# Top-32 attention and two MLPs on one core: the attention output moves from the score banks into the h banks of PSUM

## The chip, the cores and the metric

One core of one Trainium2 chip runs the whole kernel. The metric is the device time of one execution in microseconds (us); lower is better. The core's engines are named as in the profile: PE (matrix multiply; PEld is its weight load), DVE, ACT, POOL and SP, which here only issues DMAs. PSUM, the memory that PE writes, has eight banks of 512 fp32 columns on 128 partitions; SBUF is the working memory.

## The reference

For 4 batches of 8 heads, 576 tokens and head size 64:

```python
scores = (1 / sqrt(64)) * q @ k.T
kth    = the 32nd largest score of each row
scores = where(scores >= kth, scores, -1e9)
attn   = exp(scores - rowmax);  attn = attn / (attn.sum(-1) + 1e-9)
x      = attn @ v                                   # (2304 tokens, 512)
h      = x @ w_in;  g = maximum(0.01 * h, h);  y = g @ w_out
z      = maximum(maximum(y @ w1, y @ w2), y @ w3);  out = z @ w2_out
```

The first MLP is 512 to 2048 to 512, the second 512 to 768 (three times) to 512. Everything is fp32 in the reference.

## The kernel before

**Numbers.** PE works in fp16: each fp32 operand is scaled, split into a high and a low fp16 half, and each product is three matmuls (high by high, high by low, low by high). In `three` these are lines 876 to 878, in the attention output lines 833 to 835.

**Attention.** The tokens of a batch are cut into four blocks of 128 and one of 64. A step of `attention(i)` takes one block and two heads (the block of 64: four heads, laid on the two halves of the partitions), 72 steps in all. In a step:

- In two rounds, j = 0 and 1, PE writes the scores of 128 rows (one head, or two heads of the block of 64) into the tile `s` (line 718), and ACT copies them to `S` in SBUF (line 723). There is one `s` tile, so the scores of j = 1 wait for the copy of j = 0.
- DVE finds the 32nd largest score of each row: four MAX8 and three MATCH_REPLACE8 per j (lines 738, 740).
- ACT takes the exponential (788), DVE and POOL mask it (793, 797, 800), ACT and POOL split it (802, 804) into `phl`, and a DMA transposes it into `pt` (807).
- PE multiplies `pt` by `vt` (833 to 835): 30 matmuls a head pair. `vt` has a 65th column of ones, so each head gives 64 outputs and the row's sum in column 64.
- DVE adds 1e-9 to the sums, read from PSUM (line 840), and takes the reciprocal (842). ACT reads each head's 64 columns from PSUM, scales them by the reciprocal and writes them to `xs` (844). ACT and POOL split `xs` into `xhl` (850, 852).

After the last head of a block a DMA transposes `xhl` into `xu`, the input of the MLPs.

**The MLPs.** `ffn(u)` takes ten units of up to 256 tokens: an H phase (w_in, one `h` tile per 128 outputs, evacuated by ACT, line 924), accumulation with w_out in `acc`, an M phase (w1, w2, w3: three `h` tiles per 128 outputs, evacuated by ACT, line 1017, and DVE, line 1021), and accumulation with w2_out in `acc` again. The weights are unpacked and split by DVE, ACT and POOL in the first part of the kernel, beside the first attention steps.

**PSUM before.** Two banks form one tile, `sav`: the scores take columns 0 to 287 of each bank, the attention output (`av`) columns 288 to 417. Two banks are `acc`, four are `h`, which serves the H and M phases, the weight preparation and small sums (`total`, line 315).

**Order of the work.** Nothing is ordered by hand. `Plan` collects every operation with an engine, a cost, a priority and what it reads and writes, simulates the five engines and writes the instructions in the order of its start times. What the plan keeps apart are its own buffers: `s` and `av` are two buffers to it, although they lie in one tile. The semaphore waits are set afterwards, by the tile framework, from the tiles that instructions touch. The table `NB` says how many buffers a tag has; `hH`, `hM` and `hW` limit how many of the four `h` banks one phase may hold (`fbuf`). `RLAG` is a time by which the plan holds back line 840 after its input is ready.

Of the kernel before, what the change touches and what calls it, by code (L numbers as in the profile page):

```python
# [9 lines left out]
F32 = mybir.dt.float32  # L10
# [4 lines left out]
AF = mybir.ActivationFunctionType  # L15
ALU = mybir.AluOpType
# [11 lines left out]
PS = 2048.0  # L28
LNPS = float(np.log(PS))
P = 128  # L30
# [11 lines left out]
PE, ACT, DVE, POOL, SP = "PE", "ACT", "DVE", "POOL", "SP"  # L42
# [29 lines left out]
class Plan:  # L72
# [13 lines left out]
    def op(self, eng, dur, fn, r=(), w=(), pr=0.0, dma=0.0, lag=0.0):  # L86
        n = Node()
        n.eng, n.dur, n.fn, n.pr, n.dma, n.lag = eng, dur, fn, pr, dma, lag
        n.succ, n.ready, n.idx, n.eps = [], 0.0, len(self.nodes), self.eps
        deps, n.bufs = set(), []  # L90
        for k in r:
            if k in self.lastw:
                deps.add(self.lastw[k])
            self.readers.setdefault(k, []).append(n.idx)
        for k in w:
            deps.update(self.readers.get(k, ()))
            if k in self.lastw:
                deps.add(self.lastw[k])
        for k in w:
            self.lastw[k] = n.idx  # L100
            self.readers[k] = []
        deps.discard(n.idx)
        for k in list(r) + list(w):
            k = k[0] if isinstance(k, tuple) else k
            for b in (k, *k.also) if isinstance(k, Buf) else ():
                if b not in n.bufs:
                    n.bufs.append(b)
                    b.left += 1
                    b.emit += 1
        n.nd = len(deps)  # L110
        self.nodes.append(n)
        for d in deps:
            self.nodes[d].succ.append(n)
        return n
# [88 lines left out]
def act(n, psum=False, aps=0):  # L203
    return (n * 0.833 + (70 if psum else 120) + 105 * aps) / 1000
# [15 lines left out]
def attention_moe_kernel(ctx, tc, qk, v, w_in, w_out, w123, w2o, outT):  # L220
    nc = tc.nc
    V, G, A, T, Y = nc.vector, nc.gpsimd, nc.scalar, nc.tensor, nc.sync
# [3 lines left out]
    ps = ctx.enter_context(tc.tile_pool(name="ps", bufs=1, space=bass.MemoryType.PSUM))  # L226
# [2 lines left out]

    NB = {"xu": 2, "raw": 2, "hl": 1, "k2": 7, "kt": 4, "qt": 2, "vt": 4, "S": 3, "w": 1, "m": 2, "nb": 2, "pp": 1,  # L230
          "phl": 1, "pt": 1, "r": 2, "xs": 1, "xhl": 1, "f16t": 4, "yj": 1,
          "s": 1, "av": 1, "acc": 2, "h": 4, "junk": 1, "xcap": 2, "pr": 8, "ph": 4, "ra": 3, "fi": 6, "ft": 9, "rw": 3, "fz": 3, "rc": 2, "hH": 2, "hM": 3, "hW": 1, "kH": 2, "kM": 5, "fH": 2, "fM": 2}
    PSUM_TAGS = ("s", "av", "acc", "h")
    plan = Plan(NB, {"raw", "av", "junk", "hl", "k2", "h", "f16t", "rc"})
    op = plan.op
    cnt = [0]

    def buf(tag, shape, dt=F32):
        pl = ps if tag in PSUM_TAGS else sb

        def make():
            cnt[0] += 1
            if tag in ZONE:
                return ZONE[tag].pop(0)
            return pl.tile(shape, dt, tag=tag, bufs=NB[tag], name=f"{tag}_{cnt[0]}")

        b = plan.buf(tag, make)
        if tag in ZONE:
            b.done = lambda: ZONE[tag].append(b.ap)
        return b  # L250

    def fbuf(tag, ph, shape, dt=F32):
        b = buf(tag, shape, dt)
        b.also = (plan.buf({"h": "h", "k2": "k", "f16t": "f"}[tag] + ph, lambda: 1),)
        return b
# [20 lines left out]
            "ph": [wof[:, 11264 + 1152 * i:12416 + 1152 * i].rearrange("p (a s) -> p a s", a=2) for i in range(4)],  # L276
            "fz": [w2f[:, 1536 * e:1536 * e + 1536].bitcast(I32) for e in range(1, 4)]}
    NCOL = 318
    sav = ps.tile([P, 2, 512], F32, name="sav")
    ZONE["s"] = [sav[:, :, :288]]  # L280
    ZONE["av"] = [sav[:, :, 288:418]]
    colt = cp.tile([P, NCOL], F32, name="colt")
    cpos = [0]

# [392 lines left out]
        return TE + TS * i if i < NE else TA0 + TA * i  # L677

    EXPP = 4
    RLAG = 3.0  # L680
    COLD = 1.7
    NCOLD = 8
    FM = 1
# [12 lines left out]
    def attention(i):  # L696
        s = steps[i]
        b, t0, n, hps = s["b"], s["t0"], s["n"], s["hps"]
        full = n == P
        pr = TP(i)  # L700
# [42 lines left out]
        else:  # L743
# [6 lines left out]
            for x, g in [(0, 0), (0, 1), (1, 0), (0, 2), (1, 1), (0, 3), (1, 2), (0, 4), (0, 5), (0, 6)]:  # L750
# [13 lines left out]
               pr=pd)  # L764
# [46 lines left out]
        if blk not in XHL:  # L811
            XHL[blk] = buf("xhl", [P, 2, HP, P], F16)
        xhl = XHL[blk]
        xs = buf("xs", [P, 4, 64])
        avb = buf("av", [P, 512])
        av = lambda: avb().rearrange("p x (h e) -> p x h e", e=65)
        avh = lambda a: av()[:, a // 2, a % 2] if not full else av()[:, 0, a]
        for j in range(2):
            vt = VT[b, hps[j]]

            def avm(j=j, vt=vt):
                hs = [(j, slice(0, P), j)] if full else [(hh, slice(64 * hh, 64 * hh + 64), 2 * j + hh)
                                                        for hh in range(2)]
                for hh, qs, a in hs:
                    o = avh(a)[:qs.stop - qs.start, :]
                    for c in range(5):
                        if c < 4:
                            ch, k = c + 5 * j, 2 * c + hh
                        else:
# [7 lines left out]
            op(PE, 15 * mm(64) * (1 if full else 2) * (COLD if i < NCOLD else 1), avm, r=[pt] + [(vt, x) for x in range(3)], w=[avb, (xs, "a"), (xhl, "a", i)], pr=pa)  # L837
        nh = 2 if full else 4
        r = buf("r", [P, 8])
        op(DVE, 0.07, lambda: V.tensor_scalar(r()[:n, 0:nh].rearrange("p (x h) -> p x h", h=2),  # L840
                                             av()[:n, 0:nh // 2, :, 64], 1e-9 * PS, None, op0=ALU.add), r=[avb], w=[(r, 0)], pr=pr, lag=RLAG)
        op(DVE, 0.08, lambda: V.reciprocal(r()[:n, 4:4 + nh], r()[:n, 0:nh]), r=[(r, 0)], w=[(r, 1)], pr=pr)
        for h in range(nh):
            op(ACT, act(64, True, 1), lambda h=h: A.activation(xs()[:n, h], avh(h)[:n, 0:64], AF.Copy,
                                                              scale=r()[:n, 4 + h:5 + h]),
               r=[avb, (r, 1)], w=[(xs, h)], pr=pr)
        g0, gn = hps[0], 1 if full else 2
        xo = lambda x: xhl()[:n, x, g0:g0 + gn].rearrange("p g d -> p (g d)")
        xi = lambda: xs()[:n, 0:nh].rearrange("p h d -> p (h d)")
        op(ACT, act(64 * nh), lambda: A.activation(xo(0), xi(), AF.Copy), r=[(xs, h) for h in range(nh)],  # L850
           w=[(xhl, 0, g0)], pr=pr)
        op(POOL, pool(64 * nh) + 0.06, lambda: G.tensor_tensor(xo(1), xi(), xo(0), op=ALU.subtract),
# [341 lines left out]
```

## Time and profile before

| | |
|---|---|
| median of 3 runs | 1130.32 us (1129.85 to 1130.76) |
| the profiled execution | 1129.44 us, of which the span of the trace is 1127.3 us |
| PE busy | 917.1 us, 81% of the span |
| DVE busy | 972.9 us, 86% |
| ACT busy | 757.2 us, 67% |
| POOL busy | 687.1 us, 61% |

2.1 us of the profiled execution lie outside the span. Busy shares are averages over parts of the run that differ: DVE has hardly a pause while there is attention to do, and PE is loaded least at the start, where there are no MLP units yet. Matmuls are pipelined, so a busy PE is not PE at its peak.

### The profile page before, as it was taken

The page shows a single profiled execution, that of the slowest core. Times are in us where ns is not written, and L with a number is a line of the kernel's source. Part 1 is how long each engine was busy: PE and PEld are TensorE (multiplying, and loading weights), DVE is VectorE, ACT ScalarE, POOL GpSimd, SP SyncE. Part 2 cuts the span into 40 slices and gives each one's busy share as a digit, 9 for nine tenths or more (in the row PEclk, how much of TensorE's full clock was granted, in tenths as well). Part 3 has the DMA queues.
Part 4 walks back from the last instruction along what each step waited for, and adds up shares of the span by engine and source line. Part 5 has one row for each costly group of instructions (what it writes and reads, how often), then busy time and mean ns, then how long its engine had stood idle before and what let it go on. Part 6 is the DMA issues. An engine that isn't in the chain of part 4 may idle for free.

```text
span 1127.3 us, 27415 instructions
## 1 busy us (share of the span) xinstructions
PE 917.1 (81%) x10292; PEld 800.9 (71%) x10292; DVE 972.9 (86%) x2154; ACT 757.2 (67%) x1625; POOL 687.1 (61%) x1054
## 2 busy tenths in 40 slices
PE   2253236764798998998879899989999998999998
PEld 1132235753698887987768788878888887888998
DVE  3999999999899999999999899899999999995101
ACT  7578757987468666568778665685886665665342
POOL 5475657776458655568678555675887566466121
PEclk9999996875799999999999999999999999999999
DMA  8748457667334432335664423363663433432000
GB/s 297 232 120 258 150 148 211 161 177 150 81 77 103 83 87 52 82 69 143 165 164 97 82 64 72 62 157 75 153 155 77 103 62 53 79 66 53 24 1 16
DMA packets 268517, 125.79 MB, mean 112 GB/s; under 512 B 237408, under 2 KB 255328, under 8 KB 266336
## 3 DMA queue, kind: packets, MB, share of 16 engines
q1 hardware_dynamic: 268384, 124.04, 45.1%
q8 instruction: 81, 1.33, 0.5%
q14 instruction: 52, 0.43, 0.1%
HBM read 62.65 MB, written 14.16 MB: 68 GB/s over the span
## 4 chain that ended last, share of the span: by engine, by line
PE 47%; DVE 16%; ACT 11%; DMA 10%; POOL 7%; issue 6%; SPq 1%; POOLq 0%; ACTq 0%; DVEq 0%
PE h L876 8%; PE h L877 8%; PE h L878 8%; DMA pt<-phl 6%; PE acc L877 5%; PE acc L876 5%; PE acc L878 5%; PE sav L718 4%; DVE m L738 4%; DVE w L740 3%; ACT S L723 2%; PE sav L833 2%; PE sav L834 2%; PE sav L835 2%; DVE w L505 2%
## 5 line engine op out<-in xcount | busy, mean ns | idle before, releaser
L738 DVE MAX8 m<-w 128x8 f32<-128x576 f32 x432 | 309.8, 746 | 0.2 <-DVE r L840 0.2
L937 POOL TENSOR_TENSOR f16t<-k,f16t 128x256 f16<-128x256 f32 (+2 forms) x220 | 144.4, 658 | 175.5 <-ACT f16t L931 150.2
L804 POOL TENSOR_TENSOR phl<-pp,phl 128x576 f16<-128x576 f32 x144 | 184.1, 1288 | 50.5 <-ACT phl L802 49.8
L740 DVE MATCH_REPLACE8 w<-m,w 128x576 f32<-128x576 f32 x288 | 212.0, 741 | 0.0
L876 PE MATMUL h<-k,w 128*128 128x256 f16 (+2 forms) x720 | 187.2, 264 | 7.3 <-ACT k L977 4.0
L877 PE MATMUL h<-k,w 128*128 128x256 f16 (+2 forms) x720 | 187.0, 264 | 3.4 <-POOL k L979 3.3
L878 PE MATMUL h<-k,w 128*128 128x256 f16 (+2 forms) x720 | 186.9, 264 | 0.0
L877 PE MATMUL acc<-f16t,wo 128*128 128x256 f16 (+2 forms) x640 | 167.0, 265 | 5.3 <-POOL f16t L937 5.0
L876 PE MATMUL acc<-f16t,wo 128*128 128x256 f16 (+2 forms) x640 | 166.9, 265 | 0.9 <-ACT k L974 0.5
L878 PE MATMUL acc<-f16t,wo 128*128 128x256 f16 (+2 forms) x640 | 166.9, 265 | 0.0
L718 PE MATMUL sav<-kt,qt 128*128 128x288 f16 (+5 forms) x800 | 109.7, 288 | 61.9 <-ACT S L723 45.9
L876 PE MATMUL h<-xu,wi 128*128 128x256 f16 (+1 forms) x576 | 154.9, 269 | 6.1 <-DMA xu<-xhl 5.3
L877 PE MATMUL h<-xu,wi 128*128 128x256 f16 (+1 forms) x576 | 154.9, 269 | 0.0
L878 PE MATMUL h<-xu,wi 128*128 128x256 f16 (+1 forms) x576 | 154.9, 269 | 0.0
L802 ACT ACTIVATE phl<-pp 128x576 f16<-128x576 f32 x144 | 96.8, 679 | 54.4 <-DVE pp L793 22.7
L788 ACT ACTIVATE pp<-S,nb,colt 128x576 f32<-128x576 f32 x144 | 121.2, 860 | 16.9 <-POOL phl L804 9.3
L718 PEld LDWEIGHTS <-qt 128*128 128x128 f16 (+1 forms) x800 | 64.7, 109 | 87.3 <-issue 71.7
L931 ACT ACTIVATE f16t<-k 128x256 f16<-128x256 f32 (+2 forms) x220 | 85.7, 392 | 52.3 <-DVE k L1021 49.6
L800 POOL TENSOR_TENSOR pp<-pp,S 128x576 f32<-128x576 f32 x72 | 92.1, 1279 | 43.4 <-DVE S L797 32.7
L833 PE MATMUL sav<-vt,pt 128*128 128x65 f16 (+1 forms) x800 | 92.7, 203 | 29.3 <-DMA pt<-phl 22.8
L924 ACT ACTIVATE k<-h,colt 128x256 f32<-128x256 f32 (+2 forms) x160 | 71.0, 451 | 64.1 <-PE h L878 63.8
L723 ACT ACTIVATE S<-sav 128x576 f32<-128x576 f32 x144 | 92.4, 642 | 29.6 <-PE sav L718 14.5
(136 smaller groups left out, 2643.3 us busy)
## 6 DMA issues: line engine op xcount, KB each, us to landing
w<-in_w SPq DMA_DIRECT2D x18, 512.0 KB, 3.9
w<-in_w_in SPq DMA_DIRECT2D x8, 1024.0 KB, 7.2
w<-in_w_out SPq DMA_DIRECT2D x8, 1024.0 KB, 5.0
raw<-in_qk SPq DMA_DIRECT2D x24, 288.0 KB, 3.4
dqk<-hl SPq DMA_DIRECT2D x48, 144.0 KB, 2.5
kt<-dqk SPq DMA_DIRECT2D x16, 288.0 KB, 3.3
qt<-dqk SPq DMA_DIRECT2D x144, 32.0 KB, 2.2
raw<-in_v SPq DMA_DIRECT2D x12, 352.0 KB, 3.4
```

Of the source, the lines that this page charges most:

```text
L718: T.matmul(p()[osl, h, o:o + w], q()[:, hh, st, :n], k()[:, hh, kc:kc + w], start=st == 0, stop=st == 1, skip_group_check=True)
L723: op(ACT, act(S, True), lambda t=t, p=p: A.activation(t().rearrange("p (a s) -> p a s", a=2), p()[:, :, :288], AF.Copy), r=[p], w=[(Sp, j) ...
L738: op(DVE, dve(S) * 1.03, lambda mc=mc, src=src: V.max(mc(), src()), r=rd, w=[(m, j, 0, r)], pr=pd)
L740: op(DVE, dve(S) * 1.03 + 0.06, lambda mc=mc, src=src, j=j: V.match_replace(out=wj(j), in_to_replace=mc(), in_values=src(), imm_value=NEG) ...
L788: op(ACT, act(S, aps=2), lambda j=j, es=es: A.activation(pp()[:, j], Sb[j](), AF.Exp, bias=nb()[:, j:j + 1], scale=es[:, 0:1]), r=[(Sp, j) ...
L802: op(ACT, act(S), lambda j=j: A.activation(phl()[:, 0, j], pp()[:, j], AF.Copy), r=[(pp, j)], w=[(phl, 0, j)], pr=pr)
L804: op(POOL, pool(S), lambda j=j: G.tensor_tensor(phl()[:, 1, j], pp()[:, j], phl()[:, 0, j], op=ALU.subtract), r=[(pp, j), (phl, 0, j)], w= ...
L833: T.matmul(o, hc, vh, start=c == 0, stop=False, skip_group_check=True)
L876: T.matmul(out, wt(0), xt(0), start=first, stop=False, skip_group_check=True)
L877: T.matmul(out, wt(0), xt(1), start=False, stop=False, skip_group_check=True)
L878: T.matmul(out, wt(1), xt(0), start=False, stop=last, skip_group_check=True)
L937: op(POOL, pool(N) + 0.044, lambda: G.tensor_tensor(hl()[:, 1, :N], g()[:, 0, :N], hl()[:, 0, :N], op=ALU.subtract), r=[(g, 0), (hl, 0)], ...
```

## The change

The attention output gets one of the four `h` banks for as long as it needs it (a fifth kind of tenant, at most one at a time: `"hA": 1`). One ACT instruction per step copies all its columns, sums included, from PSUM to `xs`, which is now 65 columns a head. The sums (line 838 of the changed kernel) and the scaling (843) read and write `xs` in SBUF. The tile `sav` is gone, and the scores have two banks to themselves. `RLAG` goes from 3.0 to 1.5 us. A step so has one ACT instruction more, and no instruction fewer.

```diff
-          ... "hH": 2, "hM": 3, "hW": 1, "kH": 2, ...}
+          ... "hH": 2, "hM": 3, "hW": 1, "hA": 1, "kH": 2, ...}
-    sav = ps.tile([P, 2, 512], F32, name="sav")
-    ZONE["s"] = [sav[:, :, :288]]
-    ZONE["av"] = [sav[:, :, 288:418]]
...
-    RLAG = 3.0
+    RLAG = 1.5
...
-        xs = buf("xs", [P, 4, 64])
-        avb = buf("av", [P, 512])
-        av = lambda: avb().rearrange("p x (h e) -> p x h e", e=65)
-        avh = lambda a: av()[:, a // 2, a % 2] if not full else av()[:, 0, a]
+        xs = buf("xs", [P, 4, 65])
+        avb = fbuf("h", "A", [P, 512])
+        avh = lambda a: avb()[:, 65 * a:65 * a + 65]
...
-        op(DVE, 0.07, lambda: V.tensor_scalar(r()[:n, 0:nh].rearrange("p (x h) -> p x h", h=2),
-                                             av()[:n, 0:nh // 2, :, 64], 1e-9 * PS, None, op0=ALU.add), r=[avb], w=[(r, 0)], pr=pr, lag=RLAG)
+        op(ACT, act(65 * nh, True), lambda: A.activation(xs()[:n, 0:nh], avb()[:n, :65 * nh].rearrange("p (h e) -> p h e", e=65),
+                                                         AF.Copy), r=[avb], w=[(xs, h) for h in range(nh)], pr=pr)
+        op(DVE, 0.07, lambda: V.tensor_scalar(r()[:n, 0:nh], xs()[:n, 0:nh, 64:65].rearrange("p h e -> p (h e)"),
+                                             1e-9 * PS, None, op0=ALU.add), r=[(xs, h) for h in range(nh)], w=[(r, 0)],
+           pr=pr, lag=RLAG)
...
-            op(ACT, act(64, True, 1), lambda h=h: A.activation(xs()[:n, h], avh(h)[:n, 0:64], AF.Copy,
-                                                              scale=r()[:n, 4 + h:5 + h]),
-               r=[avb, (r, 1)], w=[(xs, h)], pr=pr)
+            op(ACT, act(64, False, 1), lambda h=h: A.activation(xs()[:n, h, 0:64], xs()[:n, h, 0:64], AF.Copy,
+                                                               scale=r()[:n, 4 + h:5 + h]),
+               r=[(r, 1)], w=[(xs, h)], pr=pr)
```

**What moves.** Three places show it. Rows end with the semaphores that the instruction waits for, by the engine that raises them (PE_49 is PE's, DMAHW5_49 a DMA queue's). `r` holds the sums and their reciprocals, `m` and `w` belong to the search for the 32nd score, `S` is the scores in SBUF.

DVE in a step near the middle of the kernel, where an MLP unit goes from its H to its M phase; before:

```order
L738 MAX m_1359_9390<-w_1361_9408 128x8 [waits DVE_49]
L840 TENSOR_SCALAR r_1365_9440<-sav_78 128x2 [waits PE_49,Activation_49]
L738 MAX m_1359_9390<-w_1361_9408 128x8 [waits DVE_49]
L842 RECIPROCAL r_1365_9440<-r_1365_9440 128x2 [waits DVE_49]
L740 MATCH_REPLACE w_1361_9408<-m_1359_9390,w_1361_9408 128x576
```

and with the change:

```order
L735 MAX m_1355_9507<-w_1359_9551 128x8 [waits DVE_49]
L838 TENSOR_SCALAR r_1365_9590<-xs_1357_9510 128x2 [waits Activation_49]
L735 MAX m_1355_9507<-w_1359_9551 128x8 [waits DVE_49]
L841 RECIPROCAL r_1365_9590<-r_1365_9590 128x2 [waits DVE_49]
L737 MATCH_REPLACE w_1359_9551<-m_1355_9507,w_1359_9551 128x576
```

The sum stands at the same place among the same neighbours; it no longer waits for PE, only for ACT, which now writes its input.

ACT around the same sums; before:

```order
L802 ACTIVATE phl_1358_9373<-pp_1348_9286 128x576 [waits Pool_49]
L723 ACTIVATE S_1362_9419<-sav_78 128x576 [waits DVE_49]
L931 ACTIVATE f16t_1363_9427<-k2_1360_9400 128x256 [waits Activation_49]
L723 ACTIVATE S_1362_9419<-sav_78 128x576 [waits DVE_49]
L844 ACTIVATE xs_1357_9356<-sav_78,r_1365_9440 128x64 [waits DVE_49]
L844 ACTIVATE xs_1357_9356<-sav_78,r_1365_9440 128x64 [waits PE_49]
L850 ACTIVATE xhl_1343_9225<-xs_1357_9356 128x128 [waits Activation_49]
```

and with the change:

```order
L799 ACTIVATE phl_1354_9502<-pp_1348_9439 128x576 [waits DMAHW1_49,DVE_49]
L836 ACTIVATE xs_1357_9510<-h_1356_9509 128x130 [waits PE_49,Pool_49]
L930 ACTIVATE f16t_1360_9553<-k2_1353_9496 128x256 [waits Activation_49]
L720 ACTIVATE S_1361_9559<-s_1347_9434 128x576 [waits Pool_49]
L799 ACTIVATE phl_1354_9502<-pp_1348_9439 128x576
L923 ACTIVATE k2_1363_9578<-h_1358_9547,colt_78 128x256 [waits PE_49]
L720 ACTIVATE S_1361_9559<-s_1362_9569 128x576 [waits PE_49]
L843 ACTIVATE xs_1357_9510<-xs_1357_9510,r_1365_9590 128x64 [waits DVE_49,Activation_49]
```

The copy from the `h` bank is new and stands ahead of both score copies; those no longer wait for DVE, and the second scaling no longer for PE.

PE where an attention output starts inside an M phase; before:

```order
L876 MATMUL h_1425_9905<-k2_1375_9489,w1_76 128x256 [waits DVE_49]
L833 LDWEIGHTS pt_1417_9832 [waits DMAHW5_49]
L833 MATMUL sav_78<-vt_1233_8375,pt_1417_9832 128x65
L834 LDWEIGHTS pt_1417_9832
L834 MATMUL sav_78<-vt_1233_8375,pt_1417_9832 128x64
```

and with the change:

```order
L875 MATMUL h_1426_10083<-k2_1375_9660,w1_76 128x256 [waits DVE_49]
L829 LDWEIGHTS pt_1418_10010 [waits DMAHW5_49]
L829 MATMUL h_1427_10087<-vt_1233_8518,pt_1418_10010 128x65 [waits DVE_49]
L830 LDWEIGHTS pt_1418_10010
L830 MATMUL h_1427_10087<-vt_1233_8518,pt_1418_10010 128x64
```

The place is the same; the first matmul now also waits until DVE has read the `h` tile that had the bank before.

## Rows read from the trace of the kernel before

**Rows 1.** The page, part 1: busy time and share of each engine.

```profile
PE 917.1 (81%) x10292; PEld 800.9 (71%) x10292; DVE 972.9 (86%) x2154; ACT 757.2 (67%) x1625; POOL 687.1 (61%) x1054
```

**Rows 2.** Busy us by stretch: stretch, length, engines, granted clock, DMA share, GB/s.

```profile
290.00:620.00 330.00, 301.37 (x3740) 267.87 (x3740) 310.53 (x691) 229.67 (x519) 216.42 (x331) 0.98 0.45 102
620.00:1010.00 390.00, 369.71 (x4011) 322.76 (x4010) 368.92 (x817) 263.97 (x584) 246.72 (x354) 0.99 0.42 89
1010.00:1047.00 37.00, 36.38 (x436) 32.37 (x434) 20.21 (x45) 19.91 (x49) 20.33 (x30) 1.00 0.25 57
1047.00:1127.30 80.30, 74.55 (x843) 71.92 (x840) 8.52 (x22) 27.60 (x73) 19.30 (x39) 1.00 0.05 15
```

**Rows 3.** Waits of DVE, 300 to 1010 us: us in total, times, longest us.

```profile
DVE r L840 <- PE sav L718: 12.8, 12, 2.7
DVE r L840 <- ACT S L723: 7.0, 8, 2.2
DVE r L840 <- ACT k L924: 1.3, 1, 1.3
```

**Rows 4.** Waits of PE, 300 to 1010 us.

```profile
PE sav L833 <- DMA pt<-phl: 9.5, 10, 2.7
PE sav L718 <- ACT S L723: 7.6, 14, 1.5
PE h L876 <- DMA xu<-xhl: 5.3, 1, 5.3
PE h L876 <- ACT k L1017: 3.2, 3, 1.6
...
PE sav L718 <- ACT xs L844: 2.3, 4, 1.4
...
PE sav L833 <- ACT S L723: 1.6, 2, 0.8
PE sav L718 <- DVE r L840: 1.5, 2, 1.0
```

**Rows 5.** Waits of ACT, 300 to 1010 us.

```profile
ACT k L924 <- PE h L878: 43.0, 46, 3.4
...
ACT xs L844 <- PE sav L718: 13.8, 23, 1.3
...
ACT xs L844 <- DVE r L842: 10.1, 14, 1.8
...
ACT S L723 <- DVE r L840: 7.6, 9, 1.5
```

**Rows 6.** Timeline, 641 to 647 us: start, us, engine, instruction, idle before, releaser.

```profile
642.72 0.66 PE L718 MATMUL sav<-kt,qt 128*128 128x64 f16 x6
...
643.48 0.16 DVE L840 TENSOR_SCALAR r<-sav 128x2 f32<-128x2 f32 x1 [2.65 <-PE sav L718]
...
643.67 0.65 ACT L723 ACTIVATE S<-sav 128x576 f32<-128x576 f32 x1 [1.49 <-DVE r L840]
...
645.09 0.65 PE L718 MATMUL sav<-kt,qt 128*128 128x288 f16 x4 [1.38 <-ACT xs L844]
...
645.78 0.31 ACT L844 ACTIVATE xs<-sav,r 128x64 f32<-128x64 f32 x1 [0.74 <-PE sav L718]
```

**Rows 7.** Groups of ACT by shape: count, busy us, mean ns, idle before.

```profile
L924 ACT ACTIVATE k<-h,colt 128x256 f32<-128x256 f32 x112 | 52.4, 474 | 46.6 <-PE h L878 46.5
L844 ACT ACTIVATE xs<-sav,r 128x64 f32<-128x64 f32 x128 | 34.8, 311 | 30.0 <-PE sav L718 16.8 <-DVE r L842 12.6 <-DVE m L738 0.4
...
L850 ACT ACTIVATE xhl<-xs 128x128 f16<-128x128 f32 x64 | 19.8, 310 | 0.6
...
L355 ACT ACTIVATE raw<-raw,colt 128x576 f32<-128x576 f32 x24 | 18.1, 767 | 2.9 <-POOL colt L336 2.9
...
L356 ACT ACTIVATE hl<-raw 128x576 f16<-128x576 f32 x24 | 16.2, 674 | 3.1 <-DMA dqk<-hl 3.1
...
L924 ACT ACTIVATE k<-h,colt 128x128 f32<-128x128 f32 x16 | 5.6, 364 | 1.9 <-PE h L878 1.9
```

More of the change, by code (lines that the diff above doesn't have):

```diff
@@ L231, in attention_moe_kernel @@
           "phl": 1, "pt": 1, "r": 2, "xs": 1, "xhl": 1, "f16t": 4, "yj": 1,
-          "s": 1, "av": 1, "acc": 2, "h": 4, "junk": 1, "xcap": 2, "pr": 8, "ph": 4, "ra": 3, "fi": 6, "ft": 9, "rw": 3, "fz": 3, "rc": 2, "hH": 2, "hM": 3, "hW": 1, "kH": 2, "kM": 5, "fH": 2, "fM": 2}
+          "s": 1, "av": 1, "acc": 2, "h": 4, "junk": 1, "xcap": 2, "pr": 8, "ph": 4, "ra": 3, "fi": 6, "ft": 9, "rw": 3, "fz": 3, "rc": 2, "hH": 2, "hM": 3, "hW": 1, "hA": 1, "kH": 2, "kM": 5, "fH": 2, "fM": 2}
     PSUM_TAGS = ("s", "av", "acc", "h")
@@ L839, in attention @@
         r = buf("r", [P, 8])
-        op(DVE, 0.07, lambda: V.tensor_scalar(r()[:n, 0:nh].rearrange("p (x h) -> p x h", h=2),
-                                             av()[:n, 0:nh // 2, :, 64], 1e-9 * PS, None, op0=ALU.add), r=[avb], w=[(r, 0)], pr=pr, lag=RLAG)
+        op(ACT, act(65 * nh, True), lambda: A.activation(xs()[:n, 0:nh], avb()[:n, :65 * nh].rearrange("p (h e) -> p h e", e=65),
[3 more added lines that the diff above has]
+           pr=pr, lag=RLAG)
         op(DVE, 0.08, lambda: V.reciprocal(r()[:n, 4:4 + nh], r()[:n, 0:nh]), r=[(r, 0)], w=[(r, 1)], pr=pr)
         for h in range(nh):
-            op(ACT, act(64, True, 1), lambda h=h: A.activation(xs()[:n, h], avh(h)[:n, 0:64], AF.Copy,
-                                                              scale=r()[:n, 4 + h:5 + h]),
-               r=[avb, (r, 1)], w=[(xs, h)], pr=pr)
+            op(ACT, act(64, False, 1), lambda h=h: A.activation(xs()[:n, h, 0:64], xs()[:n, h, 0:64], AF.Copy,
+                                                               scale=r()[:n, 4 + h:5 + h]),
+               r=[(r, 1)], w=[(xs, h)], pr=pr)
         g0, gn = hps[0], 1 if full else 2
-        xo = lambda x: xhl()[:n, x, g0:g0 + gn].rearrange("p g d -> p (g d)")
-        xi = lambda: xs()[:n, 0:nh].rearrange("p h d -> p (h d)")
+        xo = lambda x: xhl()[:n, x, g0:g0 + gn].rearrange("p g (h d) -> p (g h) d", h=2)
+        xi = lambda: xs()[:n, 0:nh, 0:64]
         op(ACT, act(64 * nh), lambda: A.activation(xo(0), xi(), AF.Copy), r=[(xs, h) for h in range(nh)],
```

## The prediction

> **What bounds the kernel now.** I read four views in this order: busy time, busy time by stretch, the waits of PE, DVE and ACT, and a timeline.
>
> Busy time alone names DVE: 972.9 us, against 917.1 us of PE [rows 1]. By stretch it looks different. From 290 us on, when the MLP units can run, PE is busy for 301.37 of 330 us, 369.71 of 390, 36.38 of 37 and 74.55 of 80.3 [rows 2]; its pauses are 28.6 + 20.3 + 0.6 + 5.8 = 55.3 us in all. DVE in the first two of these stretches pauses 19.5 + 21.1 = 40.6 us, and then runs out of attention: 20.2 us busy of the next 37, and 8.5 of the last 80.3, while PE works on almost without a gap. So the end is PE's. Its matrix work is not touched by the change, and what can be won is a part of its 55.3 us of pauses. What DVE wins counts only where it lets PE pause less.
>
> Who makes the pauses? On DVE, 12.8 + 7.0 + 1.3 = 21.1 of the 40.6 us stand before one tiny instruction, the sum of line 840 [rows 3]. It reads the attention output, which PE finished earlier; yet it is released by PE's next scores, or by ACT's copy of them. The timeline shows why that is dear [rows 6]: DVE stands idle for 2.65 us until PE has written scores (line 718), which the sum does not use but which lie in the same tile and banks; ACT's copy of those scores then waits 1.49 us for the sum; PE's next scores wait 1.38 us for the scaling on ACT; and the second scaling waits 0.74 us for those scores. Four instructions of two unrelated jobs take turns. In the waits of PE and ACT the same turns stand with their totals: PE 2.3 us for the scaling, 1.6 for the score copy before an attention output, 1.5 for the sum [rows 4]; ACT 13.8 us (scaling behind scores), 10.1 (scaling behind the reciprocal) and 7.6 (score copy behind the sum) [rows 5].
>
> **The change, part by part.** All sums are savings or costs on PE's path after 290 us; before that, PE waits for weights anyway and I count nothing.
>
> *The false turns go.* In the instruction order shown ahead, the sum no longer waits for PE, the score copies not for DVE, the second scaling not for PE. PE saves at once 2.3 + 1.6 + 1.5 = **5.4 us** [rows 4].
>
> *Scores behind the score copy, 7.6 us* [rows 4]. This wait is partly real: there is still one score tile, and round j = 1 needs the copy of j = 0. But the copy was itself held for 7.6 us by the sum [rows 5]. Between nothing and all of it I take half: **3.8 us**.
>
> *Attention outputs behind the transpose DMA, 9.5 us* [rows 4]. The transpose follows DVE's masks, so it comes earlier when DVE does not stand before the sum. DVE loses 21.1 us of waits [rows 3], more than the 9.5 us; but it is not shown that the late steps are those whose sums waited. Between 0 and 9.5 I take half: **4.7 us**.
>
> *The MLP input, 5.3 us once* [rows 4], is PE waiting for attention as such. Between 0 and 5.3 I take **3.0 us**, more than half, since DVE's 21.1 us begin to add up from 300 us on.
>
> Together 16.9 us, with ends of 5.4 and 27.8.
>
> *ACT gets more to do.* One copy of 130 columns on 128 partitions in 64 steps, of 260 columns on 64 partitions in 8. The nearest rows read PSUM with a scale operand: 364 ns for 128 columns, 474 for 256 [rows 7]. The scale operand costs 767 - 674 = 93 ns on 576 columns, so a plain copy takes about 273 and 385 ns: 64 x 0.273 + 8 x 0.385 = 20.6 us. The 160 scalings move from PSUM (311 ns) to SBUF: 310 ns for 128 columns without scale, less 64 columns at (474 - 364) / 128 = 0.86 ns, plus 93, makes 348 ns, so 160 x 0.037 = 5.9 us. ACT's 757 us become about 784. What covers this is ACT's idle time, 720 - 229.67 - 263.97 = 226 us between 290 and 1010 [rows 2], out of which 23.9 us were the false waits of the scaling. Without that cover the 0.27 us of each copy would fall on PE in the roughly 61 steps after 290 us: 17 us. PE's waits for an ACT instruction that evacuates `h` are 3.2 us [rows 4], so the value is near zero; I take **2 us**, ends 0 and 17.
>
> *The sum itself* (0.16 us [rows 6]) and the reciprocal stay on DVE. The sum reads SBUF instead of PSUM; for 72 of them even the whole duration would be 11.5 us, and I count nothing.
>
> *The lag falls from 3.0 to 1.5 us.* That only lets the plan put the sum closer behind the copy. At the place shown it stands between the same neighbours, and a late copy would make DVE wait there with MAX8 and MATCH_REPLACE8 behind it.
>
> *A fifth tenant in four `h` banks.* This is the new risk. In the order, 43 of the 72 attention outputs now begin with a matmul that also waits for the last reader of the bank, and some `h` tiles wait for the new copy. The row nearest to it is PE's wait for ACT's reading of an `h` tile in the M phase: three waits, 3.2 us, so 1.07 us each [rows 4]. Among many hundred tiles three waits say that the banks come free in time: near zero. At the other end, 43 x 1.07 = 46 us. I take **3 us**. The Trainium skill, "Perfetto Trace Analysis", section Optimizing Tensor Performance, speaks against this part: independent matmul groups should rotate through different PSUM banks, so that the evacuation of one overlaps the next. Taken strictly, each loan of a bank would cost a wait, and the sum would be a loss instead of a gain; the three waits shown say there is room for the rotation as it is.
>
> *Queues.* ACT's copy stands early in ACT's queue and waits for PE's last attention matmul; behind it stand a score copy, a split of `phl` and an evacuation of `h`. The copy also waits in 17 of 72 steps for POOL to have read the one `xs` buffer of the step before. SP issues the same DMAs.
>
> **Sum.** 16.9 - 2 - 3 = 11.9 us off the profiled execution's 1129.44 us: 1117.5. The median of the runs is 0.9 us above that execution, which makes **1118 us**.
>
> **The rivals.**
>
> *DVE decides (1109 us).* If attention, not PE's own waits, holds PE back, all of DVE's 21.1 us come off [rows 3]: 1130.3 - 21 = 1109. For it speaks that the MLP input and the transposes are among PE's longest waits [rows 4]; against it that PE has but 55.3 us of pauses, many without any link to the sum, and that it finishes alone.
>
> *The stalls move (1130 us).* ACT runs in order, and its evacuations of `h` already wait 43.0 us for PE in 46 waits, 0.93 us each [rows 5]. If each of some 61 copies waits like that, ACT stands 57 us more, against the 23.9 us that it gets back; score copies, exponentials and evacuations behind it come later, PE saves its 5.4 us and loses them again. Against it: ACT's 226 us of idle time [rows 2].
>
> *The bank loan decides (1141 us, slower).* In the M phase three `h` tiles are open and DVE, which reads two of them, is busy for 94% of the time [rows 2]. An attention output that waits for DVE holds up PE's whole queue. With 14.9 us of gain left before this term, the point is 14.9 / 43 = 0.35 us for each of the 43 waits; at 0.6 us each the loss is 25.8 us and the time 1130.3 + 10.9 = 1141. Against it: no wait of PE for DVE's reading of an `h` tile is among those from 300 to 1010 us. By the skill's rule on rotating banks this rival would be the likely one; the rows leave it a small chance.
>
> That the change does nothing is no rival here: the order shows the waits gone.
>
> **How the numbers follow.** My forecast, a gain of 6 to 18 us, gets 0.52; DVE deciding 0.16; stalls moving 0.17, of which 0.06 still gain a few us and 0.11 lie within 0.2% (2.3 us, about what a measurement of this kernel can tell from no change); the bank loan 0.15. So faster 0.74, same 0.11, slower 0.15. The range goes from 1105 us, a little under the DVE case, to 1132 us, above the moved stalls; what is left out is most of the bank loan (0.13) and some 0.05 below.
>
> **What would show it.** Right: DVE's waits before the sum fall from 21.1 us to a few, now released by ACT's copy; PE's waits for scaling, sum and score copy (5.4 us) vanish; PE's pauses after 290 us fall from 55 to some 43 us; ACT's busy time is 780 to 790 us; DVE runs out of attention 12 to 20 us earlier. Wrong: PE waiting for DVE or ACT before attention outputs or `h` tiles by more than 10 us (bank loan), or ACT waiting 50 us and more before the copy with PE's pauses unchanged (moved stalls). A stretch before 290 us that ends earlier or later by several us would be a part that I counted at nothing.

## The result: slower, with the predicted waits gone

The changed kernel takes **1138.08 us** (median of 6 runs, 1134.23 to 1142.01), the kernel before 1130.34 us beside it (6 runs, 1129.85 to 1131.48): the ratio is **1.0067, 95% interval 1.0045 to 1.009**. Forecast were 1118 us and a range of 1105 to 1132; the time lies above it. The profiled execution, from which the lines of this section come, took 1134.23 us, the fastest of the six: the trace shows 5.1 us of a longer span, while the medians differ by 7.7.

The page of the changed kernel, part 1, answers to [rows 1]:

```profile
PE 916.3 (81%) x10292; PEld 805.0 (71%) x10292; DVE 993.3 (88%) x2154; ACT 779.8 (69%) x1697; POOL 679.9 (60%) x1054
```

ACT's growth is the predicted one (784 forecast, 779.8 found). What no part of the change accounts for is DVE's: the same 2154 instructions, and 20.4 us more of busy time. Busy time by stretch of the changed kernel (columns as in [rows 2]) shows where it falls:

```profile
290.00:620.00 330.00, 300.91 (x3674) 267.93 (x3674) 315.77 (x691) 237.22 (x546) 212.21 (x331) 0.96 0.47 102
620.00:1010.00 390.00, 367.96 (x4054) 322.37 (x4054) 380.22 (x818) 275.07 (x616) 246.50 (x354) 1.00 0.44 90
1010.00:1047.00 37.00, 34.55 (x418) 30.71 (x416) 21.09 (x48) 22.78 (x58) 20.76 (x33) 1.00 0.25 56
1047.00:1132.40 85.40, 79.66 (x890) 76.51 (x887) 9.36 (x24) 27.34 (x71) 19.40 (x39) 0.98 0.05 14
```

DVE gains 5.2 and 11.3 us of busy time in the first two stretches. PE's pauses from 290 us on are 29.1 + 22.0 + 2.5 + 5.7 = 59.3 us, after 55.3 before; with 1.1 us more of busy time that is the 5.1 us by which the profiled span grew (1127.3 to 1132.4). At 1047 us PE has that much more left to do: 79.66 us of work, after 74.55.

The groups of instructions by shape, changed kernel (columns: busy us, mean ns of one, idle before), show where DVE's 20.4 us come from:

```profile
L838 DVE TENSOR_SCALAR r<-xs 128x2 f32<-128x2 f32 x64 | 30.8, 481 | 4.5 <-ACT xs L836 4.3
L841 DVE RECIPROCAL r<-r 128x2 f32<-128x2 f32 x64 | 9.4, 147 | 0.0
L838 DVE TENSOR_SCALAR r<-xs 64x4 f32<-64x4 f32 x8 | 2.2, 276 | 4.0 <-ACT xs L836 4.0
...
L836 ACT ACTIVATE xs<-h 128x130 f32<-128x130 f32 x64 | 17.9, 280 | 53.5 <-PE h L831 53.4
L843 ACT ACTIVATE xs<-xs,r 128x64 f32<-128x64 f32 x128 | 37.9, 341 | 13.8 <-DVE r L841 13.7
```

All sums, first before and then changed (min/median/max ns, first and last start in us):

```profile
L840 DVE TENSOR_SCALAR r<-sav x72: 131/148/160, 66.6 to 1045.8; 128x2 f32<-128x2 f32 x64, 64x4 f32<-64x4 f32 x8
```

```profile
L838 DVE TENSOR_SCALAR r<-xs x72: 141/181/1234, 64.0 to 1043.0; 128x2 f32<-128x2 f32 x64, 64x4 f32<-64x4 f32 x8
```

The sum of two numbers per partition took 150 ns on average when it read PSUM. Reading `xs` in SBUF it takes 481 ns, and all 72 sums (eight of them add four numbers) take 33.0 us instead of 10.8. The copy (280 ns) and the scaling (341 ns) on ACT cost what was worked out for them (273 and 348).

The waits between 300 and 1010 us answer to [rows 3] to [rows 5]. DVE, PE and ACT of the changed kernel:

```profile
DVE r L838 <- ACT xs L836: 5.0, 5, 2.2
```

```profile
PE h L829 <- DMA pt<-phl: 15.4, 18, 2.6
PE h L875 <- DMA xu<-xhl: 7.7, 2, 7.1
PE s L715 <- ACT S L720: 6.7, 9, 1.5
PE acc L876 <- POOL f16t L936: 5.1, 8, 1.6
...
PE h L829 <- ACT k L1016: 1.9, 1, 1.9
```

```profile
ACT xs L836 <- PE h L831: 50.3, 42, 3.3
```

The false turns did go: DVE waits 5.0 us before the sum, after 21.1, and PE waits no more for scaling or sum. But the sums between 300 and 1010 us now take 27.3 us instead of 8.5: 16.1 us of waits won were paid with 18.8 us of longer sums, and the attention on DVE came hardly earlier. Between 480 and 660 us the sums end on average 2.0 us later, step by step, than before; the last one starts 2.8 us earlier (1043.0 after 1045.8). PE's waits for transposes grew from 9.5 to 15.4 us, for the MLP input from 5.3 to 7.7, and for POOL's half of `f16t`, an input of the MLPs' accumulation, from 1.3 (the line below, of the kernel before) to 5.1.

```profile
PE acc L877 <- POOL f16t L937: 1.3, 3, 0.7
```

What stretches a sum is seen beside POOL. Timeline of the changed kernel (start, us, engine, instruction, idle before):

```profile
300.76 1.28 POOL L801 TENSOR_TENSOR phl<-pp,phl 128x576 f16<-128x576 f32 x1 [4.78 <-ACT phl L799]
301.43 0.63 DVE L838 TENSOR_SCALAR r<-xs 128x2 f32<-128x2 f32 x1
...
642.46 0.67 POOL L936 TENSOR_TENSOR f16t<-k,f16t 128x256 f16<-128x256 f32 x1
642.51 0.64 DVE L838 TENSOR_SCALAR r<-xs 128x2 f32<-128x2 f32 x1
```

Each of these sums ends when POOL's instruction ends, 0.02 us after it. Over the whole trace, 33 of the 72 sums take more than 0.25 us (26.6 us together). In all 33 a TENSOR_TENSOR of POOL was running when they began, and all 33 end 0.02 to 0.03 us after it. The 39 short ones are the counter-test in the same trace: 24 began with POOL idle and took 141 to 184 ns, 6 began beside another kind of POOL instruction and took 160 to 178 ns, and 9 began when a TENSOR_TENSOR had 0.18 us or less to go, and ended after it too.

### The profile page after: what moved, and what is told of

The parts are those of the page before. It is cut to its first block, busy times and chain, and to the rows that moved or that the text cites. A ratio compares the mean times of both kernels' runs of the same rounds, so it can differ in the third digit from the quotient of the medians.

```text
span 1132.4 us, 27465 instructions
## 1 busy us (share of the span) xinstructions
PE 916.3 (81%) x10292; PEld 805.0 (71%) x10292; DVE 993.3 (88%) x2154; ACT 779.8 (69%) x1697; POOL 679.9 (60%) x1054
## 4 chain that ended last, share of the span: by engine, by line
PE 40%; DVE 28%; DMA 10%; ACT 8%; POOL 6%; issue 6%; SPq 1%; POOLq 0%; ACTq 0%; DVEq 0%
DVE m L735 9%; DMA pt<-phl 8%; DVE w L737 8%; PE h L875 7%; PE h L876 7%; PE h L877 7%; PE acc L876 4%; PE acc L877 4%; PE acc L875 4%; PE s L715 3%; PE h L829 2%; DVE S L794 2%; POOL phl L801 1%; DVE w L502 1%; DVE acc L496 1%
## 5 line engine op out<-in xcount | busy, mean ns | idle before, releaser
L936 POOL TENSOR_TENSOR f16t<-k,f16t 128x256 f16<-128x256 f32 (+2 forms) x220 | 140.6, 641 | 188.8 <-ACT f16t L930 161.9
L715 PE MATMUL s<-kt,qt 128*128 128x288 f16 (+5 forms) x800 | 108.3, 286 | 52.3 <-ACT S L720 49.8
L829 PE MATMUL h<-vt,pt 128*128 128x65 f16 (+1 forms) x800 | 92.9, 204 | 33.5 <-DMA pt<-phl 27.5
L829 PEld LDWEIGHTS <-pt 128*128 128x128 f16 (+1 forms) x800 | 81.9, 107 | 38.7 <-DMA pt<-phl 36.1
L923 ACT ACTIVATE k<-h,colt 128x256 f32<-128x256 f32 (+2 forms) x160 | 71.0, 449 | 55.6 <-PE h L877 54.9
```

What stands on the lines that cost most here:

```text
L715: T.matmul(p()[osl, h, o:o + w], q()[:, hh, st, :n], k()[:, hh, kc:kc + w], start=st == 0, stop=st == 1, skip_group_check=True)
L829: T.matmul(o, hc, vh, start=c == 0, stop=False, skip_group_check=True)
L936: op(POOL, pool(N) + 0.044, lambda: G.tensor_tensor(hl()[:, 1, :N], g()[:, 0, :N], hl()[:, 0, :N], op=ALU.subtract), r=[(g, 0), (hl, 0)], ...
```

## The experiments

Three theories stood: the stretched sums cost the time (form); the new order of instructions costs it (order: the plan is made anew from the new durations and lag, so it moved in many more places than the three shown); the loan of a bank or the copy on ACT costs it. Ratios are to the kernel before in the same set of runs (1130.96 to 1132.23 us there). The versions with TENSOR_REDUCE leave out the addition of 1e-9.

**The form alone, order kept.** The sum as a reduction over one element, same data in SBUF, same order on every engine:

```diff
-        op(DVE, 0.07, lambda: V.tensor_scalar(r()[:n, 0:nh], xs()[:n, 0:nh, 64:65].rearrange("p h e -> p (h e)"),
-                                             1e-9 * PS, None, op0=ALU.add), ...
+        op(DVE, 0.07, lambda: V.tensor_reduce(r()[:n, 0:nh], xs()[:n, 0:nh, 64:65], axis=AX.X, op=ALU.add), ...
```

> The changed kernel with one instruction form replaced: DVE gathers the row sums from xs with a TENSOR_REDUCE over one element in place of the TENSOR_SCALAR that adds 1e-9 (the 1e-9 is left out). Same count, same inputs, same place in the order. Theory A (the TENSOR_SCALAR on SBUF is stretched by POOL's instructions): the sum falls from 0.46 us on average to about 0.15, DVE busy falls by about 22 us to 971, and the time falls by 8 to 20 us from 1138 to 1118 to 1130. Theory B (the h bank's loan, or ACT standing 61 us before its copy, costs the time): DVE busy may fall, but the time stays within 3 us of 1138. Theory C (reading SBUF is slow whatever the instruction): the sum stays at 0.4 us and more.

1128.74 us, ratio 0.9991 (0.9975 to 1.0006): 9.3 us less than the changed kernel. All instructions of line 838 in this version (min/median/max ns), and its timeline at the place shown above:

```profile
L838 DVE TENSOR_REDUCE r<-xs x72: 127/145/156, 65.3 to 1036.3; 128x2 f32<-128x2 f32 x64, 64x4 f32<-64x4 f32 x8
```

```profile
298.56 1.28 POOL L801 TENSOR_TENSOR phl<-pp,phl 128x576 f16<-128x576 f32 x1 [4.75 <-ACT phl L799]
299.24 0.14 DVE L838 TENSOR_REDUCE r<-xs 128x2 f32<-128x2 f32 x1
```

The sum runs in the middle of the same POOL instruction and takes 0.14 us. 37 of its 72 sums lie wholly within one TENSOR_TENSOR of POOL, none takes over 0.16 us. Theory A was expected to bring 1118 to 1130 us and did. It also shows what is left of the change without the long sums. Busy time by stretch:

```profile
290.00:620.00 330.00, 302.48 (x3739) 269.16 (x3739) 310.93 (x692) 236.65 (x546) 213.88 (x330) 0.97 0.46 102
620.00:1010.00 390.00, 370.15 (x4073) 325.38 (x4071) 372.74 (x826) 276.14 (x622) 247.97 (x359) 1.00 0.44 91
1010.00:1047.00 37.00, 34.56 (x398) 30.61 (x395) 14.78 (x35) 19.72 (x51) 18.57 (x28) 1.00 0.20 44
1047.00:1125.70 78.70, 72.93 (x828) 70.45 (x826) 8.38 (x21) 25.99 (x68) 18.01 (x37) 0.99 0.04 13
```

DVE's last sum starts 9.5 us earlier than before (1036.3 after 1045.8), and yet PE's pauses from 290 us on are 27.5 + 19.9 + 2.4 + 5.8 = 55.6 us, as before the change (55.3). They stand elsewhere; PE's largest waits from 300 to 1010 us in this version:

```profile
PE h L829 <- DMA pt<-phl: 14.2, 17, 2.3
PE h L875 <- DMA xu<-xhl: 7.5, 2, 7.1
PE s L715 <- ACT S L720: 6.5, 8, 1.5
PE acc L876 <- POOL f16t L936: 5.2, 9, 1.6
```

**The lag, alone and with the other form.** The changed kernel with `RLAG = 3.0` as before, then the same with the reduction:

> The changed kernel with the lag of the sum back at 3.0 us, nothing else. Theory A (stretched sums): no difference beyond 3 us, the sums still take 0.4 to 0.5 us on average. Theory D (the sum stands too close behind the copy): DVE's 8.3 us of waits before the sum go and the time falls by 4 us or more. A different order by the plan alone can move the time by a few us either way.

> The lag-3.0 version of the changed kernel (1144 us), same order on all engines, with TENSOR_REDUCE in place of TENSOR_SCALAR for the sum. Theory A: 8 to 14 us faster, 1130 to 1136. Theory B (order alone): 1141 to 1147.

1144.01 us, ratio 1.0119 (1.0083 to 1.0155), and 1135.18 us, 1.0033 (1.0019 to 1.0047). The form is worth 8.8 us in this order too; the order is worse than that of 1.5 with either form. The first of the two expectations missed: it had no difference, or a gain, for the longer lag.

**The bank loan without the copy.** Attention output in the `h` bank, sums and scaling read it there:

```diff
-        op(ACT, act(65 * nh, True), ... A.activation(xs()[:n, 0:nh], avb() ..., AF.Copy), ...
-        ... V.tensor_scalar(r()[:n, 0:nh], xs()[:n, 0:nh, 64:65] ...
+        ... V.tensor_scalar(r()[:n, 0:nh], avb()[:n, :65 * nh].rearrange("p (h e) -> p h e", e=65)[:, :, 64], ...
-            ... A.activation(xs()[:n, h, 0:64], xs()[:n, h, 0:64], AF.Copy, ...
+            ... A.activation(xs()[:n, h, 0:64], avh(h)[:n, 0:64], AF.Copy, ...
```

> Only the move of the attention output into the h bank: no copy; the sum and the scalings read the h bank in PSUM as they read the score banks before. Theory A (the SBUF sum is the loss, the false waits were a real cost): sums at 0.15 us, DVE busy near 973, false waits gone, time 1110 to 1125. Theory B (the bank's loan costs): the bank is now held longer (copy gone, sum, reciprocal and scalings in its place), so the time is as slow as the changed kernel or slower, 1138 to 1150. If the false waits cost nothing in truth: 1127 to 1133.

1131.43 us, ratio 1.0002 (0.9983 to 1.002), though this bank is held longer. The sums are short here (146 ns in the middle, 160 at most), the false turns are gone and there is no copy; that is the third of the expected cases, in which the false waits cost nothing in truth, though in this order only. Its PE waits from 290 to 1010 us:

```profile
PE h L829 <- DMA pt<-phl: 18.4, 18, 2.7
...
PE h L873 <- ACT k L1014: 3.7, 3, 2.5
```

Waits for transposes lead here as well (11.6 us before, in the same window); PE's wait for ACT's reading of an `h` tile, 3.2 us in [rows 4], is 3.7 us.

**The copy kept, the sum from PSUM.** One line, beside the copy:

```diff
-        ... V.tensor_scalar(r()[:n, 0:nh], xs()[:n, 0:nh, 64:65] ..., r=[(xs, h) for h in range(nh)], ...
+        ... V.tensor_scalar(r()[:n, 0:nh], avb()[:n, :65 * nh].rearrange("p (h e) -> p h e", e=65)[:, :, 64], ..., r=[avb], ...
```

> The changed kernel, but the sum reads column 64 of each head from the h bank in PSUM, beside the copy; the scalings still read xs. Theory A (SBUF sum stretched): sums back at 0.15 us, DVE busy near 973, time 1115 to 1130. Theory B (ACT's copy and its wait, 61 us, hold others up): time stays near 1138.

**1115.37 us, ratio 0.9876 (0.9845 to 0.9908)**: below both kernels, and 2.6 us off the forecast of 1118.

```profile
L838 DVE TENSOR_SCALAR r<-h x72: 133/146/160, 64.2 to 1035.6; 128x2 f32<-128x2 f32 x64, 64x4 f32<-64x4 f32 x8
```

The same operation that took up to 1234 ns on SBUF takes 160 at most on PSUM. But its plan is another one, so form and order are mixed. The next two keep this plan and put back the sums from SBUF (where the copy stands ahead of the sum, 68 of 72), once as reduction, once as TENSOR_SCALAR:

> The instruction order of the run that sums from PSUM (1115 us), engine by engine, but 68 of the 72 sums read xs in SBUF with a TENSOR_REDUCE; the 4 sums that stand ahead of their copy still read the h bank. Theory A (only the TENSOR_SCALAR form on SBUF is stretched; the order makes the rest of the difference): sums at 0.15 us, time 1112 to 1121. If reading the sum from SBUF itself costs, or the wait for the copy: 1125 and more.

> The same order again, with the changed kernel's TENSOR_SCALAR from xs in those 68 steps. Theory A: sums at 0.4 us and more on average, DVE busy about 20 us more than with the TENSOR_REDUCE, and a time 7 to 15 us above that run. Theory B (what the changed kernel lost lies in its order alone): equal to it within 3 us.

1118.89 us, 0.9894 (0.9877 to 0.991), and 1123.51 us, 0.9944 (0.9924 to 0.9965), with these sums:

```profile
L841 DVE TENSOR_REDUCE r<-xs x68: 125/146/158, 64.3 to 1033.9; 128x2 f32<-128x2 f32 x60, 64x4 f32<-64x4 f32 x8
```

```profile
L841 DVE TENSOR_SCALAR r<-xs x68: 149/196/1221, 63.1 to 1035.0; 128x2 f32<-128x2 f32 x60, 64x4 f32<-64x4 f32 x8
```

The form is worth 4.6 us in this order, less than the 7 to 15 expected. And with the reduction in both, the two orders differ by 1128.7 - 1118.9 = 9.8 us.

**The kernel before with the new lag,** `RLAG = 1.5` and nothing else:

> The kernel before with the lag of the sum at 1.5 instead of 3.0 us, nothing else. Theory of the false turns: the sum is put closer behind the attention output, so it more often stands behind scores or score copies of the shared banks in the same way; DVE's wait before the sum stays at 20 us or grows, time 1128 to 1140. If the lag were what the change gains by, the time falls below 1127.

1146.56 us, ratio 1.0138 (1.0117 to 1.0159). A number that only the plan reads costs 16 us, more than any of the expected cases; PE's wait for transposes (290 to 1010 us) goes from 11.6 to 22.1 us:

```profile
PE sav L833 <- DMA pt<-phl: 22.1, 23, 3.2
```

**Where the two orders part.** Their count of MLP matmuls runs apart between 550 and 600 us. Busy time from 560 to 620 us, first the reduction in the changed kernel's order, then in that of the faster one:

```profile
560.00:620.00 60.00, 50.65 (x637) 43.24 (x636) 56.92 (x124) 47.79 (x105) 44.79 (x69) 0.91 0.59 132
```

```profile
560.00:620.00 60.00, 58.96 (x732) 51.58 (x730) 58.46 (x126) 49.65 (x109) 47.55 (x75) 1.00 0.60 136
```

PE pauses 9.35 us against 1.04. In the first, one wait is 7.1 us, for the transpose of the MLP input `xu`; SP's queue in its timeline shows it issued behind a transpose of `pt` and four stores of the finished unit, in the other order ahead of them:

```profile
574.16 3.10 SPq L804 DMA_TRANSPOSE pt<-phl  x1
577.31 2.03 SPq L1058 DMA_DIRECT2D out_T<-k  x4
579.43 1.24 SPq L869 DMA_TRANSPOSE xu<-xhl  x1
```

So the next edit puts these five behind it, with every other engine's order unchanged (in the plan's `run`, behind its sorting; `kind` marks the DMAs of `xu` and `out_T`):

```diff
-        for _, i in order if self.EMIT else ():
-            n = self.nodes[i]
+        seq = [self.nodes[i] for _, i in order]
+        for x in [n for n in seq if n.kind == "xu"]:
+            q = seq.index(x)
+            ahead = [m for m in seq[:q] if m.eng == SP][-5:]
+            if len([m for m in ahead if m.kind == "out"]) == 4:
+                for m in ahead:
+                    if not any(n in m.succ for n in seq[:q]):
+                        seq.remove(m)
+                        seq.insert(seq.index(x) + 1 + ahead.index(m), m)
+        for n in seq if self.EMIT else ():
```

> The changed kernel with one edit on SP's queue: at the one place where the transpose of the MLP input xu stands behind a transpose of pt and four DMAs of out_T, those five are issued just behind it instead; the order of PE, DVE, ACT and POOL is the same. Theory A (the place of this one DMA in SP's queue makes the whole difference of order): PE's wait of 7.1 us for xu shrinks to 3 us or less, and the time falls by 5 to 9 us, from about 1138 to 1129 to 1133. Theory B (the 7.1 us are only where a lateness of the attention work shows; the difference of order lies elsewhere): PE waits later for pt or scores what it no longer waits for xu, and the time stays within 3 us, 1135 to 1141.

> The kernel with the sum by TENSOR_REDUCE from SBUF (1128.74 us) and the same edit on SP's queue. Theory A: 5 to 9 us off, 1119.5 to 1124, near the 1118.9 us of the same sums in the other order, and within the range about the predicted 1118. Theory B: 1126 to 1131, as without the edit.

> The kernel before with the same edit on SP's queue; there PE waits 5.3 us for xu. Theory A: 3 to 6 us off, 1125 to 1128. Theory B: 1129 to 1132. Between them: if the kernel before gains nothing and the changed one does, the lateness of xu counts only with the banks separated.

1136.26 us, 1.0035 (1.0017 to 1.0053); 1131.35 us, 0.9983 (0.9964 to 1.0003); 1131.27 us, 0.9989 (0.9976 to 1.0003). By the ratios that is 3.6, 0.9 and 1.2 us less than without the edit, the last two within the intervals: theory A, which had 5 to 9 us for the first two and 3 to 6 for the third, falls. The reduction's PE waits from 560 to 620 us, with the edit, tell why:

```profile
PE h L884 <- DMA xu<-xhl: 2.5, 1, 2.5
PE h L837 <- DMA pt<-phl: 2.1, 2, 1.4
PE s L723 <- DMA qt<-dqk: 1.3, 2, 1.0
```

`xu` was issued 6.9 us earlier (at 572.52 us; the whole queue was 1.9 us ahead by then), but what stood behind it in the queue became late in its place: 7.1 + 0.8 us for `xu` and `pt` became 2.5 + 2.1, and 1.3 for `qt` came on top. The faster order differs there on PE as well, which has MLP work of the unit before left to fill the stretch.

**Is it the lag, the bank, or chance?** The last four vary the lag in both forms with short sums.

> The kernel with the sum by TENSOR_REDUCE from SBUF, RLAG 1.05 instead of 1.5: the sum is planned 1.05 us behind the copy, about the distance from PE's end at which the version that sums from the bank plans it. Three readings of the order's 10 us stand. C (scatter: the plan is thrown into another order by any small change, and the times of the orders differ by some us up and down): anything between 1115 and 1145, with no trend over the lags. D (a sum planned nearer to the attention output is better): 1117 to 1123. B (a bank that the plan holds for the sum as well as for the copy is better): 1126 to 1131, as with 1.5.

> The same with RLAG 2.0. The same form measured 1128.74 at 1.5 and 1135.18 at 3.0. C: anything between 1115 and 1145. D: between those two, 1129 to 1134. B: 1126 to 1135.

> The version that sums from the h bank beside the copy (1115.37 at RLAG 1.5), with RLAG 1.0. C: anything between 1110 and 1145. D: 1115 or less. B: 1113 to 1118.

> The version that sums from the h bank beside the copy, with RLAG 3.0. C: anything between 1110 and 1145. D: 1122 or more, as the sums from SBUF lose 6.4 us from 1.5 to 3.0. B: 1113 to 1120.

1129.27, 1127.04, 1123.11 and 1136.06 us. All ratios, by lag of the plan (the 95% intervals reach 0.0014 to 0.0036 to either side):

| sum | 1.0 (1.05) | 1.5 | 2.0 | 3.0 |
|---|---|---|---|---|
| as before (no copy, shared bank) | | 1.0138 | | 1 |
| TENSOR_SCALAR from SBUF | | 1.0067 | | 1.0119 |
| TENSOR_REDUCE from SBUF | 0.9979 | 0.9991 | 0.9953 | 1.0033 |
| TENSOR_SCALAR from PSUM, with copy | 0.9928 | 0.9876 | | 1.0037 |

D falls: nearer sums are not steadily better (0.9979 at 1.05, 0.9953 at 2.0), and before, 3.0 is the better lag; of its four forecasts only that for the sum from PSUM at 3.0 came true. B falls: the version that holds the bank is at 1.0037 with 3.0. What is left is C, by elimination: with the work fixed, orders lie up to 1.6% apart. In the row of TENSOR_REDUCE the times go with PE's pauses: from 290 us on these are 58.6, 55.6, 52.4 and 60.6 us by lag, and PE's wait for transposes (290 to 1010 us) is 17.5, 14.2, 9.4 and 18.8. The long lag is the worst in each row with a copy and the best in the row without; no run tells why, and whether the sum from PSUM leads to better orders than the reduction (it does at 1.0 and 1.5, by 0.5 and 1.2%) is open.

## Why the prediction was wrong

**The step that failed: "The sum itself ... reads SBUF instead of PSUM; for 72 of them even the whole duration would be 11.5 us, and I count nothing".** It bounded the sum's cost by its old duration, and so left out that the duration could change with the place of its operand. It went from 10.8 to 33.0 us, all on the engine that feeds the transposes. Three pairs of runs with one order each price this at 9.3, 8.8 and 4.6 us of time. That is the loss against the kernel before: without it the change stands at a ratio of 0.9991.

The trace of the kernel before had shown such a hold, on a larger instruction: the mask of line 797, also a TENSOR_SCALAR from SBUF (min/median/max ns).

```profile
L797 DVE TENSOR_SCALAR S<-S,m x72: 478/516/1140, 40.4 to 1025.8; 128x576 f16<-128x576 f32 x72
```

The 44 that began with no TENSOR_TENSOR of POOL running took 478 to 521 ns. Of the 28 that began beside one, 24 ended 0.315 to 0.319 us after it did, and took up to 1140 ns. Of the other four, three began when it had 0.15 us or less to go, and one was not held.

The Trainium skill, "SBUF — State Buffer", section Who interferes with whom, has the rule that spoke against the change and that the prediction missed: DVE and GpSimd (POOL in the profile) share one pair of SBUF ports as an exclusive lock; when DVE works in a two-port mode, whichever starts first blocks the other for its whole instruction; `tensor_scalar` can enter such a mode, `tensor_reduce` on trn2 never contends. The Trainium skill, "VectorE: DVE Perf Modes", section Why PSUM operands drop a tier, adds that an operand in PSUM keeps an instruction out of the two-port modes. The traces agree where they bear on it: 33 of 72 sums from SBUF held until POOL's TENSOR_TENSOR ends, up to 1234 ns; over all runs 166 ns at most with TENSOR_REDUCE, 189 from PSUM. No run shows a port, so that this is the reason rests on the Trainium skill; the holding and its two cures are shown.

**The second: the pauses of PE, which were to fall from 55 to some 43 us, and the order.** With the sums mended the forecast 11.9 us are still missing: the false waits are gone and DVE runs out of attention 9.5 us earlier (12 to 20 were forecast), but PE pauses for 55.6 us as before. "That the change does nothing is no rival here: the order shows the waits gone" was the wrong inference: a wait that goes can come back as another one. In another order the same sums leave 47.5 us of pauses and take 1118.9 us, so whether PE gets the gain depends on the order. "At the place shown it stands between the same neighbours" was true there and said nothing of the other 71 steps; "SP issues the same DMAs" was true and left out their order. The lag was called a matter of the plan only; alone, in the kernel before, it costs 16 us. The prediction had no term for the plan's scatter, which in the runs with short sums spans 0.9876 to 1.0037, some 18 us, more than the forecast gain. The range was too narrow by it. That the sum from PSUM came within 2.6 us of 1118 is therefore luck of its order: with the lag at 1.0 and 3.0 it takes 1123.1 and 1136.1 us.

**Point by point.**

- *False turns, 5.4 us*: right. PE's waits for scaling and sum are gone, DVE's waits before the sum fell to 5.0 us.
- *Scores behind the copy, 3.8 of 7.6 us*: not won. From 300 us on 6.7 us are left, but from 290 us on it is 9.8 us after 8.9 before.
- *Transposes, 4.7 of 9.5 us, and MLP input, 3.0 of 5.3*: wrong in sign, 15.4 and 7.7 us. With short sums in the same order they are still 14.2 and 7.5, so most of the growth is not the sums'. In the faster order with the same sums the wait for the MLP input is gone and that for transposes is still 13.5; over the four lags with TENSOR_REDUCE the latter goes from 9.4 to 18.8. "DVE loses 21.1 us of waits" did not bring PE's waits down by itself; why a given order has more of them is not shown.
- *A wait that the prediction does not name*: PE for POOL's half of `f16t`, 5.1 us after 1.3, and 5.2 with short sums.
- *ACT, 2 us*: duration right (the 93 ns for a scale operand came from two rows that differ in their output type as well, but the copy and the scaling came out near it), and no wait of PE for ACT grew much. The "stalls move" rival had the waits before the copy right (57 us forecast, 53.4 + 7.6 = 61 us found by groups), and PE's pauses did not fall, so its sign was met. But these waits did not set the time: with 61.8 us of them the sum from PSUM takes 1115 us, and the version without a copy pauses for 56.1 us and takes 1131.
- *Bank loan, 3 us*: about right, 1.9 us of PE's wait for ACT's reading before an attention output, and 0.4 us each for DVE's reading there and for the new copy. The slower side was forecast by a mechanism that did not act; it came by another.
- *DVE decides*: not all of what DVE wins comes off. In the three pairs DVE's sums shrink by 21 to 23 us and the time by 4.6 to 9.3.

## What to carry to other kernels

When an operand of a small DVE instruction moves from PSUM to SBUF, ask which form the instruction has and what POOL does beside it: here a TENSOR_SCALAR of two elements took as long as POOL's TENSOR_TENSOR had to go, a TENSOR_REDUCE or a PSUM source did not. Look for the same form elsewhere in the trace of before: one that takes twice its usual time beside POOL is a warning. Where a planner writes the order, a change of one duration or lag reorders the whole program; separate what an edit does from what its plan does by runs that hold the order still, and expect the plan alone to move the time by as much as the edit.

## What the runs showed that was not expected

- A two-element TENSOR_SCALAR on SBUF took 141 to 1234 ns, while the reciprocal behind it, on the same two elements in SBUF, stayed at 147 ns on average (group of line 841 above), and at 163 at most where it ran inside a TENSOR_TENSOR of POOL (41 of 72). No run tells what sets these two apart.
- PE's granted clock averaged 0.91 (1.00 is 2.4 GHz) between 560 and 620 us with 9.35 us of pause, and 1.00 with 1.04 us (the two stretches above).
- An input DMA that is issued 6.9 us earlier on SP was worth 0.9 to 3.6 us, of which at most the 3.6 are clear of noise: the instructions it passes in the queue have users too.
